# Heads 4 to 7 with the halves of a chunk exchanged over the partitions, in a DeltaNet and SiLU kernel

## The chip, the core and the metric

The kernel runs on one core of a Trainium2 chip. TensorE (PE; its weight loads are listed as PEld), VectorE (DVE), ScalarE (ACT) and GpSimd (POOL) compute, SyncE (SP) issues the DMAs. The metric is the device time of one execution in microseconds. Three runs of the kernel before gave 767.76, 767.8 and 769.63 us, with a median of 767.8 us.

## What is computed

First a recurrent attention block, then a two-layer network on its output. With 4 batches, 8 heads, 768 tokens and head size 48:

```python
k_n = k / (np.linalg.norm(k, axis=-1, keepdims=True) + 1e-06)
for t in range(S):
    y[:, :, t] = q_t @ state                 # state: (B, H, 48, 48)
    v_old = state^T @ k_n_t
    state = state + beta_t * outer(k_n_t, v_t - v_old)
x = y.transpose(0, 2, 1, 3).reshape(3072, 384)
h = x @ w_in                                 # 384 -> 2048
return (h * sigmoid(h)) @ w_out              # 2048 -> 384
```

Everything is in 4-byte floating point.

## The kernel before, in words

**Chunks.** The 768 tokens are cut into 6 chunks (`c`) of 128 tokens. A chunk of one batch (`x`, 0 to 3) is a unit, with all its 8 heads (`h`). Token t of the chunk lies on partition t: the first half of a chunk on partitions 0 to 63 (`lo`), the second on 64 to 127 (`hi`). Within a chunk the recurrence becomes a triangular system over 128 tokens for each head. Its inverse is built from the inverses of the 32x32 blocks on the diagonal (`invert`, L441, a chain of 60 VectorE operations over all heads of a chunk at once, and DMAs before and after it), which `merge` (L526) joins to inverses of 64x64 blocks (`xis`), one for each half. What lies between the halves is applied as a 64x64 product.

**Loads.** `load_k` (L122), `load_q` (L126) and `load_v` (L130) bring one unit with one DMA each, 192 KB, of rows of 192 bytes. All DMAs are issued by SP, in an order fixed in the program (`in_line`). In the built program a DMA also waits until the one eight places before it has landed.

**Scores.** `prepare` (L889) transposes keys and queries (L364), makes the products of all keys with all keys and queries (`score`, L376), scales and masks them into `ap` (ScalarE L397, VectorE L403, with the mask `above`), sends the 32x32 blocks on the diagonal out by four DMAs per unit (`block_out`, L415) and back in by one (`block_in`, L435), scales the keys into `bkb` on GpSimd, loads the keys of the unit that takes this place next, and scales the values on GpSimd.

**Solve.** `solve(c, us)` (L508) is where the change lies. It is a generator. After each of its steps the main loop (from L1047) puts a piece or two of the network of the chunk before it in TensorE's order, so that the one waits while the other computes. `pin` fixes the order of each engine's instructions to that of the program. The steps are:

- `keys(x)` (L551) for the four units, in one step: the product of the old state with the keys. The two heads of a pair lie on the rows 0 to 63 and 64 to 127 of `kq` and of the state, which is block-diagonal, so that one 128x128 product with 96 columns serves both. Four of them fill one PSUM bank `ph` from the pool `psC` (three banks), and VectorE adds it to the values `vs` (L563). In the first chunk there is no old state and no such step.
- `merge`, first and second, a step each.
- Seven rounds, k = 0 to 6. Round k takes `inner(k, lo)` (8 products of 64x64 with 48 columns, rows lo to rows lo), `across(k-1)` (8, rows lo to rows hi) and `inner(k-2, hi)` (8, rows hi to rows hi), as far as these units exist, one product of each in turn (`together`). So rounds 0 to 5 have 8, 16, 24, 24, 16 and 8 products. Each product appears in the profile as two instructions, two passes. After the products: `add(k-1)` on VectorE (64x384), `keep(k)` and `keep(k-2)` on ScalarE (64x384 each, from PSUM into `z`). From round 3 on the round also takes the unit k-3 through `old`, `update` (the new state, L615 and L622) and `new` (the output, L632, L668, L681).

In the main loop `squares` (L284) and `norms` (L301) of the chunk after stand between rounds: after step n = 5 and n = 6, that is after rounds 2 and 3. `norms` is a chain of 15 small VectorE operations (L308 to L326). It gives `n` (what the values are multiplied by) and `g` (what the keys are). The main loop takes two pieces after the two merge steps and one after every other.

**Network.** `hidden` (L724) and, from the second chunk on, `combine` (L810), which makes two 128-token products of the second layer from seven half-size ones; `sum_g` (L798) makes its sums on VectorE, three operations at a time (S3, S4) when `combine` has come to that place. In the first chunk `project` (L748) takes the place of `combine`.

Of the kernel before, what the change touches and what calls it, by code (L numbers as in the profile page):

```python
# [21 lines left out]
def kernel(  # L22
# [91 lines left out]

    def packed(t):
        return t[:].rearrange("p a e w -> p (a e) w")[:, :, 0:D]
# [4 lines left out]

    def load_k(i):  # L122
        if i < N:
            in_line(nc.sync.dma_start(out=packed(kbufs[i % NK]), in_=chunk_of(k, i)))
# [5 lines left out]
    def load_v(i):  # L130
        if i < N and i not in vfs:
            vfs[i] = load.tile([P, H, D], FP32, name="vf", bufs=4)
            in_line(nc.sync.dma_start(out=vfs[i][:], in_=chunk_of(v, i)))
# [118 lines left out]
    )  # L252
    for t in states[: B - 1]:
        nc.gpsimd.memset(t[:], 0.0)
# [21 lines left out]
    def beta_of(c):  # L276
        pb = bank(psA, "a", "pb")
        pin(nc.tensor.transpose(pb[:, 0:BH], beta_fm[:, c * C : (c + 1) * C], ident[0:BH, 0:BH]))
        pin(nc.scalar.activation(out=beta_tok[:, c, :], in_=pb[:, 0:BH], func=ACTF.Copy))
# [21 lines left out]
    def norms(c):  # L301
# [5 lines left out]
        n, g = (small.tile([P, BH], FP32, name=name) for name in ("n", "g"))  # L307
        pin(nc.vector.tensor_scalar(  # L308
# [14 lines left out]
        pin(nc.vector.tensor_scalar(out=n[:], in0=t, scalar1=1e-6, scalar2=None, op0=ALU.add))  # L323
        pin(nc.vector.reciprocal(out=r, in_=n[:]))
# [3 lines left out]
        ))  # L328
        sizes[c], steps[c] = n, g
# [46 lines left out]
    def score(i, u, rooms):  # L376
# [5 lines left out]
        for g, room in enumerate(rooms):  # L382
# [10 lines left out]
            for e in range(2):  # L393
# [7 lines left out]
                for n, (h, at) in enumerate(heads):  # L401
                    j = 1 if n < by_act else 0
                    masked = pin(nc.vector.scalar_tensor_tensor(  # L403
                        out=ap[:, h, j:2, :],
                        in0=pa[e][:, at + j * C : at + 2 * C].rearrange(
                            "p (j t) -> p j t", j=2 - j
                        ),
                        scalar=bt[:, h : h + 1],
                        in1=above[:].unsqueeze(1).to_broadcast([P, 2 - j, C]),
                        op0=ALU.mult, op1=ALU.mult,  # L410
                    ))
# [96 lines left out]
    def solve(c, us):  # L508
# [42 lines left out]
        def keys(x):  # L551

            ph = bank(*CC, "ph")
            for p in range(NP):
                st = states[x][:, p, :].rearrange("p (e w) -> p e w", e=2)[:, :, 0:D]
                pin(nc.tensor.matmul(  # L556
                    ph[:, 2 * D * p : 2 * D * (p + 1)], lhsT=us[x]["kq"][:, p, 0, :], rhs=st,
                    start=(p == 0), stop=True, skip_group_check=True,
                ))
            add(x, slice(0, P), ph[:, 0:DM].rearrange("p (h d) -> p h d", h=H))  # L560

        def add(x, rows, what):
            pin(nc.vector.tensor_tensor(  # L563
                out=vs[x][rows], in0=vs[x][rows], in1=what[rows], op=ALU.add
            ))

        def inner(x, rows):

            if rows == lo:
                pzs[x] = bank(*CC, "pz")[:, 0:DM].rearrange("p (h d) -> p h d", h=H)  # L570
            for h in range(H):
                yield pin(nc.tensor.matmul(  # L572
                    pzs[x][rows, h, :], lhsT=xis[x // HB][rows, x % HB * H + h, :],
                    rhs=vs[x][rows, h, :], start=True, stop=True,
                ))

        def across(x):

            for h in range(H):
                yield pin(nc.tensor.matmul(  # L580
                    pzs[x][hi, h, :], lhsT=us[x]["ap"][lo, h, 0, W:C],
                    rhs=z_of(x)[lo, h // 2, h % 2, 0:D], start=True, stop=True,
                ))
# [5 lines left out]
        def keep(x, rows):  # L589
            pin(nc.scalar.copy(  # L590
                z_of(x)[rows, :, :, 0:D], pzs[x][rows].rearrange("p (a e) d -> p a e d", e=2)
            ))
            if c == 0:
                to = slab[x][rows, D:].rearrange("p (g w) -> p g w", g=2)[:, :, 0 : 2 * (D + GAP)]
                pin(nc.scalar.copy(
                    to.rearrange("p g (h w) -> p g h w", h=2)[:, :, :, 0:D],
                    pzs[x][rows].rearrange("p (g h) d -> p g h d", g=2)[:, :, 1:3, :],
                ))

# [88 lines left out]
        if c > 0:  # L688
            yield
# [7 lines left out]
        for k in range(B + 3):  # L697
# [3 lines left out]
            if k >= 3:  # L701
# [4 lines left out]
                    k < B and inner(k, lo), 0 <= k - 1 < B and across(k - 1),  # L706
                    0 <= k - 2 < B and inner(k - 2, hi),
                ) if part
            ))
            if 0 <= k - 1 < B:  # L710
                add(k - 1, hi, pzs[k - 1])
            if k < B:
                keep(k, lo)
            if 0 <= k - 2 < B:
                keep(k - 2, hi)
# [320 lines left out]
    for n, _ in enumerate(solve(1, us)):  # L1036
        go(pieces, 2 if n in (1, 2) else 1)
        if n == 5:
            squares(2)
        if n == 6:  # L1040
# [6 lines left out]
    for c in range(1, NCH):  # L1047
        if c + 1 < NCH:
# [13 lines left out]
            for n, _ in enumerate(solve(c + 1, us)):  # L1062
                go(pieces, 2 if n in (1, 2) else 1)
                if n == 5 and c + 2 < NCH:
                    squares(c + 2)
                if n == 6 and c + 2 < NCH:
# [36 lines left out]
```

## Time and profile before

| | |
|---|---|
| median of the runs | 767.8 us (767.76 to 769.63) |
| span of the profiled execution, first to last instruction | 766.0 us |
| outside of the span, against the median | 1.8 us |
| TensorE busy | 730.7 us, 95% of the span |
| VectorE busy | 420.2 us, 55% |
| ScalarE busy | 247.2 us, 32% |
| GpSimd busy | 84.4 us, 11% |
| mean granted TensorE clock | 0.981 of full speed |

The profile gives the profiled execution no time of its own but its span; the time around it is taken from the runs. "Busy" counts overlapping instructions once. The mean duration of an instruction is longer than the distance between two starts, since matmuls overlap: a chain of waits, which gives each instruction the time until the next begins, shows the distance. In it "issue" is time in which the engine waited for nothing that the profile shows. A clock of 1.00 is full speed.

### The profile page before, as it was taken

How to read it: one execution, taken by the hardware profiler on the slowest of the kernel's cores; microseconds unless marked ns; L12 is line 12 of the kernel's file. 1: busy time of each engine (PE TensorE's matmuls, PEld its weight loads, DVE VectorE, ACT ScalarE, POOL GpSimd, SP SyncE). 2: the span in 40 equal slices, each digit the busy share in tenths (PEclk: the TensorE clock that was granted, in tenths of full speed). 3: DMA queues.
4: the chain of work that ended last, by engine and by line, in shares of the span. 5: the costliest groups of instructions: out<-in, count | busy, mean ns of one | idle time of the engine just before them, and what ended most of it. 6: DMA issues, size and time to landing. Idle time of an engine off the chain costs nothing.

```text
span 766.0 us, 16569 instructions
## 1 busy us (share of the span) xinstructions
PE 730.7 (95%) x6806; PEld 631.0 (82%) x6806; DVE 420.2 (55%) x1090; ACT 247.2 (32%) x552; POOL 84.4 (11%) x95
## 2 busy tenths in 40 slices
PE   7489899899999999999999999999999999999998
PEld 5256687477778999898999988999987999999987
DVE  6889687872445853555763455673455672321212
ACT  5434466121444122434112434212425212322020
POOL 4005337100021000030000021000012000000000
PEclk9779799999999999999999999999999999999999
DMA  9797445131154022144012044122043013010000
GB/s 176 147 202 218 140 148 109 35 89 20 28 102 79 16 85 34 22 106 80 18 76 43 20 104 78 23 77 43 8 95 67 15 49 70 8 37 1 21 1 21
DMA packets 156283, 51.91 MB, mean 68 GB/s; under 512 B 141840, under 2 KB 148752, under 8 KB 156208
## 3 DMA queue, kind: packets, MB, share of 16 engines
q1 hardware_dynamic: 156208, 50.85, 29.0%
q8 instruction: 54, 0.88, 0.5%
q14 instruction: 21, 0.17, 0.1%
HBM read 34.70 MB, written 14.16 MB: 64 GB/s over the span
## 4 chain that ended last, share of the span: by engine, by line
PE 81%; DVE 10%; DMA 3%; ACT 2%; issue 2%; SPq 1%; POOL 1%; ACTq 0%; DVEq 0%
PE phid L730 31%; PE px L824 13%; PE py L824 11%; PE pa L387 5%; PE pz L572 4%; PE po L753 3%; DVE x L469 3%; DVE rank L465 3%; PE ph L556 2%; PE pt L364 2%; PE pyc L632 2%; PE py L540 2%; PE px L540 2%; PE pyc L604 1%; PE pu L615 1%
## 5 line engine op out<-in xcount | busy, mean ns | idle before, releaser
L730 PE MATMUL phid<-xT,w_in 128*128 128x256 f32 x1152 | 260.7, 382 | 2.2 <-ACT gT L740 1.6
L730 PEld LDWEIGHTS phid<-xT,w_in 128*128 128x128 f32 x1152 | 215.0, 190 | 37.0 <-issue 6.3
L740 ACT ACTIVATE gT<-phid 128x512 f32<-128x512 f32 x96 | 57.2, 597 | 188.7 <-PE phid L730 148.3
L403 DVE SCALAR_TENSOR_TENSOR ap<-pa,g,above 128x128 f32<-128x128 f32 x192 | 58.1, 376 | 41.6 <-ACT ap L397 41.6
L469 DVE TENSOR_TENSOR x<-x,rank 128x30 f32<-128x30 f32 (+9 forms) x180 | 59.7, 332 | 7.4 <-ACT x L458 1.1
L465 DVE TENSOR_TENSOR rank<-g,x 128x30 f32<-128x30 f32 (+9 forms) x180 | 59.4, 330 | 5.0
L806 DVE TENSOR_TENSOR sums_of_g<-gT 128x384 f32<-128x384 f32 (+1 forms) x60 | 29.3, 510 | 58.3 <-ACT gT L740 47.5
L824 PE MATMUL py<-w_out,sums_of_g 128*128 128x192 f32 x320 | 56.8, 329 | 0.0
L824 PE MATMUL px<-sums_of_w,sums_of_g 128*128 128x192 f32 x320 | 56.8, 329 | 0.0
L824 PEld LDWEIGHTS px<-sums_of_w,sums_of_g 128*128 128x128 f32 x320 | 52.2, 190 | 1.4 <-issue 1.4
L824 PEld LDWEIGHTS py<-w_out,sums_of_g 128*128 128x128 f32 x320 | 52.2, 190 | 0.4
L397 ACT ACTIVATE ap<-pa,g 128x128 f32<-128x128 f32 x144 | 41.5, 368 | 30.7 <-PE pa L387 29.7
L426 POOL MEMSET x<- 128x1024 f32 x6 | 5.7, 952 | 405.0 <-DMA xT<-part 403.5
L387 PE MATMUL pa<-kq 48*128 48x256 f32 x384 | 49.7, 390 | 0.2 <-DVE ap L403 0.2
L572 PEld LDWEIGHTS pz<-vf,xi 64*64 64x64 f32 x768 | 38.1, 142 | 13.3 <-issue 7.3
L753 PE MATMUL po<-w_out,gT 128*128 128x384 f32 x128 | 44.7, 495 | 2.9 <-POOL w_out L174 2.9
L572 PE MATMUL pz<-vf,xi 64*64 64x48 f32 x768 | 42.7, 227 | 4.9 <-DVE vf L563 4.4
L387 PEld LDWEIGHTS pa<-kq 48*128 48x128 f32 x384 | 36.2, 186 | 11.5 <-issue 7.8
L563 DVE TENSOR_TENSOR vf<-vf,ph 128x384 f32<-128x384 f32 x20 | 11.1, 554 | 53.1 <-PE ph L556 53.1
L753 PEld LDWEIGHTS po<-w_out,gT 128*128 128x128 f32 x128 | 23.4, 190 | 18.4 <-POOL w_out L174 4.1
L590 ACT COPY z<-pz 64x384 f32<-64x384 f32 x48 | 22.6, 472 | 46.2 <-PE pz L572 40.1
L563 DVE TENSOR_TENSOR vf<-vf,pz 64x384 f32<-64x384 f32 x24 | 13.4, 557 | 42.1 <-PE pz L580 26.1
(134 smaller groups left out, 955.4 us busy)
## 6 DMA issues: line engine op xcount, KB each, us to landing
kb<-in_k_dram SPq DMA_DIRECT2D x24, 192.0 KB, 3.1
z<-in_q_dram SPq DMA_DIRECT2D x24, 192.0 KB, 3.7
vf<-in_v_dram SPq DMA_DIRECT2D x24, 192.0 KB, 3.9
out_dram<-o SPq DMA_DIRECT2D x24, 192.0 KB, 2.0
w_out<-in_moe_w_in_dram SPq DMA_DIRECT2D x4, 768.0 KB, 6.3
blocks<-ap SPq DMA_DIRECT2D x96, 32.0 KB, 1.7
g<-blocks SPq DMA_DIRECT2D x24, 128.0 KB, 2.5
up<-x SPq DMA_DIRECT2D x6, 512.0 KB, 2.6
```

Of the source, the lines that this page charges most:

```text
L387: u["last"] = pin(nc.tensor.matmul(pa[e][:, pp * 2 * C : (pp + 1) * 2 * C], lhsT=kq[rows, 2 * g + pp, 0, :], rhs=kq[rows, 2 * g + pp, :, : ...
L397: copied = pin(nc.scalar.activation(out=ap[:, h, 0, :], in_=pa[e][:, at : at + C], func=ACTF.Copy, scale=bt[:, h : h + 1],))
L403: masked = pin(nc.vector.scalar_tensor_tensor(out=ap[:, h, j:2, :], in0=pa[e][:, at + j * C : at + 2 * C].rearrange("p (j t) -> p j t", j= ...
L465: pin(nc.vector.tensor_tensor(out=tv, in0=g[:, 0:m, m : m + 1].to_broadcast([P, m, n]), in1=x[:, m : m + 1, m + 1 : T].to_broadcast([P, m, ...
L469: yield pin(nc.vector.tensor_tensor(out=x[:, 0:m, m + 1 : T], in0=x[:, 0:m, m + 1 : T], in1=tv, op=ALU.add))
L540: pin(nc.tensor.matmul(pm[to, at : at + T], lhsT=left, rhs=right, start=True, stop=True))
L572: yield pin(nc.tensor.matmul(pzs[x][rows, h, :], lhsT=xis[x // HB][rows, x % HB * H + h, :], rhs=vs[x][rows, h, :], start=True, stop=True,))
L730: pin(nc.tensor.matmul(ph[:, j * GT : (j + 1) * GT], lhsT=w_in[:, a, (2 * f + j) * P : (2 * f + j + 1) * P], rhs=xTs[c, hf][:, a, :], star ...
L740: pin(nc.scalar.activation(out=gTs[f // FG][:, f % FG, :], in_=ph[:], func=ACTF.Silu, scale=0.5))
L753: pin(nc.tensor.matmul(po[:, 0:DM], lhsT=gTs[f // 2 // FG][:, f // 2 % FG, at : at + C], rhs=w_outs[f // HFF][:, f % HFF, :], start=(f == ...
L806: pin(nc.vector.tensor_tensor(out=sums_of_g[:, k, fs], in0=of[0], in1=of[1], op=op))
L824: pin(nc.tensor.matmul(to, lhsT=at, rhs=quarter(f, *b) if isinstance(b, tuple) else sums_of_w[b][:, f], start=start and f == 0, stop=f == ...
```

## The change

Heads 4 to 7 keep keys and values with the two halves of the chunk exchanged over the partitions: their first half is on hi, their second on lo. So "first half" (slot 0) is on lo for heads 0 to 3 and on hi for heads 4 to 7, and slot 1 the other way. `load_k` takes three DMAs per unit and `load_v` four in place of one each. Queries stay as they were. `beta_of` makes four small products in place of one transpose, `norms` three more copies (since `n` is needed in the order of the values, by slots, and `g` in that of the keys), and GpSimd makes a turned mask once. `keys` becomes 16 products of 64x64 with 48 columns per unit, over the four quarters of the array (48 rows lo or hi, columns lo or hi), into two banks, and two VectorE additions of 128x192; its four units are spread over two steps. In a round `inner(k, 0)` and `inner(k-2, 1)` take four heads lo to lo and four hi to hi, `across` four lo to hi and four hi to lo. `add` is one operation of 128x192, and `keep` two copies of 64x192 on ScalarE. `squares` and `norms` move by one step, with the two merges and what is taken after them, so they stay after rounds 2 and 3.

```diff
     def load_k(i):
         if i < N:
-            in_line(nc.sync.dma_start(out=packed(kbufs[i % NK]), in_=chunk_of(k, i)))
+            to = packed(kbufs[i % NK])
+            for s, rows, tokens in ((0, slice(0, P), slice(0, P)), (1, lo, hi), (1, hi, lo)):
+                in_line(nc.sync.dma_start(
+                    out=to[rows, HS * s : HS * (s + 1)], in_=part_of(k, i, s, tokens)
+                ))
...
     def load_v(i):
         if i < N and i not in vfs:
             vfs[i] = load.tile([P, H, D], FP32, name="vf", bufs=4)
-            in_line(nc.sync.dma_start(out=vfs[i][:], in_=chunk_of(v, i)))
+            for slot, rows in ((0, lo), (0, hi), (1, lo), (1, hi)):
+                tokens = hi if slot else lo
+                in_line(nc.sync.dma_start(
+                    out=slots(vfs[i])[rows, slot],
+                    in_=part_of(v, i, int((rows == lo) == (slot == 1)), tokens),
+                ))
...
+        pin(nc.vector.tensor_copy(out=n[0:W], in_=root_of[0:W]))
+        to, of = (x.rearrange("p (b s h) -> p b s h", s=2, h=HS) for x in (n[W:P], root_of[W:P]))
+        for s in range(2):
+            pin(nc.vector.tensor_copy(out=to[:, :, s], in_=of[:, :, 1 - s]))
         sizes[c], steps[c] = n, g
...
-                        in1=above[:].unsqueeze(1).to_broadcast([P, 2 - j, C]),
+                        in1=above_turned[:, j:2, :] if g == 1 else
+                        above[:].unsqueeze(1).to_broadcast([P, 2 - j, C]),
...
         def keys(x):
 
-            ph = bank(*CC, "ph")
+            phs = [bank(*CC, f"ph{e}")[:, 0 : HM].rearrange("p (n d) -> p n d", n=NP) for e in range(2)]
             for p in range(NP):
-                st = states[x][:, p, :].rearrange("p (e w) -> p e w", e=2)[:, :, 0:D]
-                pin(nc.tensor.matmul(
-                    ph[:, 2 * D * p : 2 * D * (p + 1)], lhsT=us[x]["kq"][:, p, 0, :], rhs=st,
-                    start=(p == 0), stop=True, skip_group_check=True,
+                for e, half in ((0, 0), (1, 1), (0, 1), (1, 0)):
+                    rows, cols = slice(W * e, W * e + D), slice(W * half, W * (half + 1))
+                    pin(nc.tensor.matmul(
+                        phs[e][cols, 2 * (p // 2 ^ half) + p % 2, :], lhsT=us[x]["kq"][rows, p, 0, cols],
+                        rhs=states[x][rows, p, W * e : W * e + D],
+                        start=True, stop=True, skip_group_check=True,
+                    ))
+            for e in range(2):
+                to = vs[x][:].rearrange("p (n e) d -> p n e d", e=2)[:, :, e]
+                pin(nc.vector.tensor_tensor(out=to, in0=to, in1=phs[e], op=ALU.add))
...
+        BY_TILE = (0, 4, 1, 5, 2, 6, 3, 7), (4, 0, 5, 1, 6, 2, 7, 3)
...
+        def inner(x, slot):
+
+            if slot == 0:
+                pzs[x] = bank(*CC, "pz")[:, 0:DM].rearrange("p (s h d) -> p s h d", s=2, h=HS)
+            for h in BY_TILE[slot]:
+                rows = half_of(h, slot)
+                yield pin(nc.tensor.matmul(
+                    place(pzs[x][rows], h, slot), lhsT=xis[x // HB][rows, x % HB * H + h, :],
+                    rhs=place(slots(vs[x])[rows], h, slot), start=True, stop=True,
+                    skip_group_check=True,
+                ))
+        def across(x):
+
+            for h in BY_TILE[0]:
+                rows, cols = half_of(h, 0), half_of(h, 1)
                 yield pin(nc.tensor.matmul(
-                    pzs[x][hi, h, :], lhsT=us[x]["ap"][lo, h, 0, W:C],
-                    rhs=z_of(x)[lo, h // 2, h % 2, 0:D], start=True, stop=True,
+                    place(pzs[x][cols], h, 1), lhsT=us[x]["ap"][rows, h, 0, cols],
+                    rhs=z_of(x)[rows, h // 2, h % 2, 0:D], start=True, stop=True,
+                    skip_group_check=True,
                 ))
...
+        def keep(x, slot):
+            for s in range(2):
+                rows = half_of(HS * s, slot)
                 pin(nc.scalar.copy(
+                    packed(z_of(x))[rows, HS * s : HS * (s + 1)], pzs[x][rows, slot]
                 ))
...
         for x in range(B if c > 0 else 0):
             keys(x)
-        if c > 0:
-            yield
+            if x % 2 == 1:
+                yield
...
-                go(pieces, 2 if n in (1, 2) else 1)
-                if n == 5 and c + 2 < NCH:
+                go(pieces, 2 if n in (2, 3) else 1)
+                if n == 6 and c + 2 < NCH:
                     squares(c + 2)
-                if n == 6 and c + 2 < NCH:
+                if n == 7 and c + 2 < NCH:
                     norms(c + 2)
```

## The prediction

> **What bounds the kernel now.** First the page: the span, the slices of TensorE and of its clock.
>
> ```profile
> span 766.0 us, 16569 instructions
> ...
> PE   7489899899999999999999999999999999999998
> ...
> PEclk9779799999999999999999999999999999999999
> ```
>
> From about 165 us on TensorE is full at full clock. Only before that do other things decide. The table by stretches tells it for the solve of chunks 1 and 2:
>
> ```profile
> 178.00:218.00 40.00, 40.00 (x687) 31.07 (x686) 17.64 (x48) 12.82 (x30) 0.00 (x0) 1.00 0.10 24
> ...
> 290.00:333.00 43.00, 42.05 (x738) 38.85 (x737) 22.48 (x60) 15.08 (x36) 0.00 (x0) 1.00 0.14 28
> ```
>
> TensorE is busy for 40.00 of 40.00 and 42.05 of 43.00 us, so what is taken off TensorE here comes off the end, except where it then waits. The chain of waits through the solve of chunk 2 gives the prices (start, time until the next link):
>
> ```profile
> 290.70 3.54 PE ph L556 x32
> ...
> 305.44 1.06 PE pz L572 x16
> 306.50 1.50 PE px L824 x8
> ...
> 309.06 1.50 PE py L824 x8
> ...
> 311.63 1.51 PE py L824 x8
> ...
> 324.25 0.57 DVE vf L563
> 324.82 0.04 issue
> 324.87 1.13 PE pz L572 x16
> ```
>
> The keys of four units take 3.54 us, 111 ns for each of 32 passes. Round 0 (16 passes in one quarter of the array) takes 1.06; round 1 (32 passes in two quarters) runs from 308.00 to 309.06, also 1.06; round 2 (48 passes, three quarters) from 310.56 to 311.63, 1.07. So quarters run beside each other, and a round lasts as long as its fullest quarter: 16 passes, whose starts in the timeline lie 58 ns apart (0.93), and 0.13 of tail. The piece before costs 1.50 where 8 such passes cost 1.30 elsewhere in the chain: 0.20 for going into small products. At round 5 the chain leaves TensorE: VectorE's addition for unit 3 ends late, and by the timeline TensorE waits 1.14 us for it.
>
> **The change part by part.**
>
> *Rounds.* Rounds 0 and 5 spread 16 passes over two quarters, rounds 1 and 4 spread 32 over four: 8 in the fullest. 8 x 58 ns + 0.13 = 0.60 in place of 1.06, 0.46 less. Rounds 2 and 3 keep 16 in lo-lo and in hi-hi, and gain nothing. Four rounds are 1.84 per chunk, 9.2 in chunks 1 to 5. That four quarters keep the 58 ns of three is not in the trace: below, 58 ns is the least that any row shows for such a pass, and above it is 116, if only two run at once. I take 58, as two and three did not differ.
>
> Against this the Trainium skill ("TensorE: Matmul & The Clock Gate", Part 3: Packing small matmuls) states that weight loads overlap running products only where the row groups differ. Here L572 and L580 of round 1 share the rows lo and still had 32 passes in the time of 16, so the row decides; by the rule rounds 1 and 4 would gain nothing, the keys' passes would take twice as long, and the time would be 774.4. The skill ("TensorEngine Tiling (Array Packing)", Gotcha 1) also says that different row tiles can't use one PSUM bank at once, as rounds 0 and 5 now do; the merge L540 does that in its bank, with 128 passes in 2.14 us, and by the rule the time would be 764.6.
>
> *Keys.* 32 passes per unit in four quarters are 8 x 58 = 0.46. But each unit now takes two of the pool's three banks: by the waits of the built program the second product of unit 1 waits for VectorE's first addition of unit 0, and unit 3 for unit 2. In the rows of before an addition starts as the last product ends. From the last weight load of a unit: 0.09 to its product, 0.22 of product (219 ns), 0.35 of addition (352 ns, the 64x192 form L622; before 553), 0.06 to the next load (324.81 to 324.87): 0.72, of which 0.7 is idle. A visit is then 0.20 + 0.46 + 0.7 + 0.46 + 0.13 = 1.95, two are 3.9, against 3.54: 0.3 more per chunk (rounded down, as a few products of unit 1 start before the wait), **+1.5** in five. Without the stall two visits are 2.5, a gain of 1.0 per chunk; with VectorE late by another 0.3 it is a loss of 0.9.
>
> *VectorE between rounds 2 and 5.* Chunk 2 before:
>
> ```profile
> 313.94 1.01 DVE L297 TENSOR_REDUCE ss<-sq 128x8 f32<-128x384 f32 x2 [1.61 <-ACT sq L294]
> ...
> 316.59 0.56 DVE L563 TENSOR_TENSOR vf<-vf,pz 64x384 f32<-64x384 f32 x1
> ...
> 319.45 1.36 DVE L806 TENSOR_TENSOR sums_of_g<-gT 128x384 f32<-128x384 f32 x3
> 320.73 0.17 DVE L308 TENSOR_SCALAR seed<-ss 128x32 uint32<-128x32 uint32 x1
> ```
>
> The extra step moves the pieces one round earlier. In the built order S3 (1.36) then stands ahead of the squares, in the 1.61 us that VectorE idles. That takes 1.36 off the chain before round 5. Against it: three copies in `norms` (0.19 to 0.23 each by its neighbours), 0.6; the addition itself 0.2 less; ScalarE's four copies of 0.31 (the 64x192 copy L595, 0.312) where two took 0.97, 0.27 later, but the squares no longer wait for the `o` copy, so they start 0.4 earlier. Followed from the end of round 2 (311.63), unit 3's addition ends at +12.0 instead of +13.18, TensorE arrives at +11.64 instead of +12.1: a wait of 0.4 in place of 1.14, 0.7 less in chunks 2, 3 and 4, **-2.1**. In chunk 1 no S3 exists; the addition ended 0.6 before TensorE came (210.41 against 211.0). The chain gets 0.95 longer (0.27 twice, 0.6, less 0.2), TensorE 0.46 earlier: a new wait of 0.8, **+0.8**. In chunk 5 `norms` is absent. Queued behind that addition on VectorE are only the state and `xT` copies.
>
> *Start.* SP's first issues and the queue of chunk 1's values:
>
> ```profile
> 1.25 2.79 SPq L124 DMA_DIRECT2D kb<-in_k_dram  x4
> ...
> 108.43 7.33 SPq L133 DMA_DIRECT2D vf<-in_v_dram  x4
> 115.87 2.44 SPq L431 DMA_DIRECT2D blocks<-ap  x4
> ...
> 134.58 1.78 SPq L431 DMA_DIRECT2D blocks<-ap  x4
> ```
>
> An issue that is not held up takes 0.45 (L431, four in 1.78). Twelve key loads are 5.4 in place of 2.79, ahead of the queries. But keys landed 1.18 apart by bytes, which don't change, against 1.35 for three issues: the last keys, the queries and all behind them come about **+0.7** later (0.3 to 1.2). Both the norms and the queries' transposes hang on it.
>
> *Values of chunk 1.* 16 loads follow three big ones. Numbers 9 to 16 wait for the landing of 1 to 8, about 116, so SP is free near 119.6 instead of 115.87. Unit 3's blocks waited until 134.58 for VectorE; three units of 4 issues, a landing, one issue and three key loads (about 5.1 each) put them near 135.5: **+0.9** (0 to 3) on the inverse of chunk 1, which ends the chain there. Later SP needs about 5 of the 5.6 us between units (blocks at 344.48 and 350.06), and the inverse has some 3.6 us of slack, since its last `xe` load lands near 408.4 and the merge starts at 411.99: 0, and up to 1 per chunk if that cover is gone.
>
> *Chunk 0.* Rounds 0 to 3 hide behind VectorE's weight work; rounds 4 and 5 gain 0.46 each, partly taken back by the same work. I take **-0.4** (0 to -1.1).
>
> *The rest at nothing:* beta's products run where TensorE idles 6.80 us behind L279; the masks keep size and count (L403, 376 ns); the four GpSimd copies end, at 0.3 each (the 128x128 select, 0.29), near 6.7, before the mask is needed at 13.73. `keep`'s extra 0.15 lies behind a piece of 1.3.
>
> **Sum:** -9.2 + 1.5 - 2.1 + 0.8 + 0.7 + 0.9 - 0.4 = -7.8. From the span of 766.0 that is 758.2; the median of the runs is 1.8 above the span, so **760.0**.
>
> **Rivals.**
>
> 1. *The keys don't stall*, if VectorE frees the bank before it is needed. For it: VectorE sits idle ahead of each key addition (0.34 us by the timeline). Against: the wait is in the program. Gain 1.0 in place of loss 0.3, five times: 753.5.
> 2. *SP sets the pace.* 48 more key and 72 more value issues, at 0.45 each 54 us on a queue that carries the inverse's transfers. For: SP is ordered, and each unit's blocks stand behind key loads. Against: the slack above. With 1 us per chunk and 3 at chunk 1: about 766.
> 3. *Four quarters run two at a time* (the other side). For: no row shows four. Against: two and three cost the same. Rounds 1 and 4 then stay at 1.06 (+4.6), and a unit's keys take 16 x 58 = 0.93, two visits 5.8 (+9.8 against the forecast): 774.4. It decides from 90 ns per pass on: 240 passes of the fullest quarter (five chunks of 32 + 16) times 32 ns eat the 7.8.
> 4. *The change does not do what it says*, its gains going into waits of the same solve (VectorE at round 5 in all chunks): 767.8.
>
> **How the numbers follow.** Forecast 0.66 (756 to 765), rival 1 0.13, rival 2 0.08, rival 3 0.08, rival 4 0.05. 0.3% (2.3 us) is what a measurement can tell from no change. Faster, below 765.5: forecast, rival 1 and half of rival 2, 0.83; within: the other half and rival 4, 0.09; slower: rival 3, 0.08. The range goes down to rival 1 with a little more from chunk 0, 752.5, and up to rival 2, 766.
>
> **What would show it.** Rounds 0, 1, 4 and 5 of chunks 1 to 5 at 0.60; rounds 2 and 3 at 1.06; two key visits near 1.75 to 1.95, each with one idle stretch of 0.7 released by VectorE; the wait at round 5 near 0.4 in chunks 2 to 4, and a new one in chunk 1; the first scores 0.7 later; the restart after the inverse of chunk 1 later than 164.8. It is wrong if passes in a quarter lie more than 58 ns apart with four running, or if merges wait for `xe` or `xi`.

## The result, and the profile after

The kernel after takes 800.0 us (median of four runs, 796.9 to 801.0), the kernel before 767.8 us on the same chip: a ratio of 1.041, 95% interval 1.039 to 1.044. The change makes it 4.1% slower, where 760.0 (752.5 to 766) was forecast. The profiled execution took 796.9 us, 1.7 of them outside its span. Its page, with the rows that were read first for the kernel before:

```profile
span 795.2 us, 17917 instructions
...
PE   6747899888999699999799999899999999999998
...
PEclk7868899999999899999989999999999999999999
```

TensorE is no longer full: beside a worse start it has holes in slices 14, 20 and 26, one per chunk, and the clock dips in slices 14 and 21. To see where the 29 us went, each span is cut at TensorE's first score product (the start of `prepare`) and at its first keys product (the start of `solve`) of each chunk, read off the timelines. "One load" is the experiment e1 and "e12" the last one, both below:

| stretch, us | before | after | one load | e12 |
|---|---|---|---|---|
| to the first scores | 11.3 | 14.9 | 11.2 | 12.5 |
| chunk 0, to the scores of chunk 1 | 95.4 | 104.3 | 92.5 | 96.2 |
| chunk 1, scores to keys | 71.2 | 76.8 | 71.6 | 71.8 |
| solve of chunk 1 (keys to next scores) | 45.9 | 44.4 | 44.4 | 44.4 |
| chunk 2, scores to keys | 66.8 | 74.7 | 66.9 | 67.6 |
| solve of chunk 2 | 49.6 | 47.2 | 47.3 | 47.6 |
| chunk 3, scores to keys | 66.8 | 74.5 | 66.9 | 66.9 |
| solve of chunk 3 | 49.6 | 47.3 | 47.3 | 47.4 |
| chunk 4, scores to keys | 66.8 | 72.0 | 66.9 | 66.9 |
| solve of chunk 4 | 49.6 | 47.3 | 47.3 | 47.2 |
| chunk 5, scores to keys | 66.8 | 66.9 | 66.9 | 66.9 |
| keys of chunk 5 to the end | 126.2 | 124.8 | 124.8 | 124.8 |
| the span (the rows are rounded) | 766.0 | 795.2 | 753.9 | 760.2 |

So the part that the change is about does what was forecast: the five solves (the last of them in the last row) are 10.0 us shorter. The loss, 39 us, lies where no product was changed, between the start and the solve of chunk 1 (18) and between scores and keys of chunks 2 to 4 (21). The table by stretches shows the same for chunk 2, first of the kernel after (columns: stretch, its length, then busy time and instructions of PE, PEld, DVE, ACT and POOL, then clock, DMA share and GB/s), then of the kernel before:

```profile
240.50:315.20 74.70, 68.54 (x376) 60.57 (x375) 40.87 (x118) 19.69 (x47) 8.55 (x10) 0.95 0.32 68
315.20:362.40 47.20, 46.36 (x875) 42.21 (x874) 24.29 (x72) 17.16 (x46) 1.64 (x3) 1.00 0.17 34
```

```profile
223.70:290.50 66.80, 66.80 (x375) 59.47 (x375) 41.35 (x118) 19.92 (x47) 8.14 (x10) 1.00 0.33 75
```

Nearly the same instructions, but TensorE idles for 6.2 of the 74.7 us, and the clock falls to 0.95 with it, which goes with the rest of the 7.9. TensorE's and ScalarE's timelines of the kernel after give the wait (start, duration, what, and in brackets the idle time ahead of it):

```profile
261.63 9.44 PE L792 MATMUL phid<-xT,w_in 128*128 128x256 f32 x43
277.23 4.30 PE L886 MATMUL px<-w_out,gT 128*128 128x192 f32 x16 [6.16 <-ACT gT L802]
```

```profile
265.93 0.60 ACT L802 ACTIVATE gT<-phid 128x512 f32<-128x512 f32 x1 [1.99 <-PE phid L792]
276.08 0.60 ACT L505 COPY x<-g 128x128 f32<-128x128 f32 x2 [9.55 <-DMA kb<-in_k_dram]
276.59 1.08 ACT L802 ACTIVATE gT<-phid 128x512 f32<-128x512 f32 x2
```

TensorE waits for `gT`, which ScalarE makes from TensorE's own products. ScalarE could make it at once, but works in order, and ahead of it stands a copy that begins the inverse (L505), which waits 9.55 us for the blocks `g`. (The row names a key load; the load of `g` for the last unit was issued at 273.36, just ahead of those keys, and is what the copy reads; in e4, below, the same wait of that copy, 6.65 us, is put down to `g` itself.) In the kernel before the copy and the product came without such a wait:

```profile
250.27 0.64 ACT L458 COPY x<-g 128x128 f32<-128x128 f32 x2 [0.45 <-DMA g<-blocks]
254.21 2.76 PE L824 MATMUL px<-w_out,gT 128*128 128x192 f32 x16
```

The blocks are late because of SP. Its timeline in chunk 2, after and then before:

```profile
240.93 10.70 SPq L152 DMA_DIRECT2D vf<-in_v_dram  x16
...
252.39 3.21 SPq L478 DMA_DIRECT2D blocks<-ap  x4
256.81 0.32 SPq L486 DMA_DIRECT2D g<-blocks  x1
257.24 1.78 SPq L139 DMA_DIRECT2D kb<-in_k_dram  x3
259.11 2.03 SPq L478 DMA_DIRECT2D blocks<-ap  x4
```

```profile
222.88 3.41 SPq L133 DMA_DIRECT2D vf<-in_v_dram  x4
...
228.07 1.99 SPq L431 DMA_DIRECT2D blocks<-ap  x4
231.65 0.32 SPq L439 DMA_DIRECT2D g<-blocks  x1
232.08 0.39 SPq L124 DMA_DIRECT2D kb<-in_k_dram  x1
```

16 value loads hold SP for 10.70 us, 0.67 each, where 4 took 3.41. TensorE's first score came 16.7 us later than before (240.5 against 223.75), the first blocks 24.3 (252.39 against 228.07). And behind each unit's blocks three key loads take 1.78 in place of 0.39. Then the blocks of a unit follow each other by 5.5 to 6.7 us, as far apart as the scores themselves (5.6 before), so SP never makes up for the late start.

### The profile page after: what moved, and what is told of

Same layout as the page of the kernel before. It is cut to its first block, busy times and chain, and to the rows that moved or that the text cites. A ratio compares the mean times of both kernels' runs of the same rounds, so it can differ in the third digit from the quotient of the medians.

```text
span 795.2 us, 17917 instructions
## 1 busy us (share of the span) xinstructions
PE 733.1 (92%) x7328; PEld 624.4 (79%) x7328; DVE 413.6 (52%) x1128; ACT 253.1 (32%) x596; POOL 85.3 (11%) x99
## 4 chain that ended last, share of the span: by engine, by line
PE 58%; DMA 2%; SPq 2%; issue 1%; ACT 0%; DVE 0%; DVEq 0%
PE phid L792 20%; PE px L886 14%; PE py L886 10%; PE pa L433 3%; PE pyc L694 2%; PE pyc L666 2%; PE pz L631 2%; PE pt L410 1%; PE py L587 1%; PE px L587 1%; DMA blocks<-ap 1%; PE ph L604 1%; PE pu L677 1%; SPq L478 1%; SPq L139 1%
## 5 line engine op out<-in xcount | busy, mean ns | idle before, releaser
L868 DVE TENSOR_TENSOR sums_of_g<-gT 128x384 f32<-128x384 f32 (+1 forms) x60 | 29.2, 509 | 56.4 <-ACT gT L802 46.0
L449 DVE SCALAR_TENSOR_TENSOR ap<-pa,g,above 128x128 f32<-128x128 f32 x96 | 30.2, 377 | 43.4 <-ACT ap L443 43.4
L433 PE MATMUL pa<-kq 48*128 48x256 f32 x384 | 51.4, 402 | 0.3 <-DVE ap L449 0.2
L886 PE MATMUL px<-w_out,gT 128*128 128x192 f32 x160 | 33.9, 374 | 14.2 <-ACT gT L802 14.2
L611 DVE TENSOR_TENSOR vf<-vf,ph 128x192 f32<-128x192 f32 x40 | 12.4, 351 | 61.4 <-PE ph L604 41.7
L886 PEld LDWEIGHTS px<-w_out,gT 128*128 128x128 f32 x160 | 31.2, 221 | 15.7 <-ACT gT L802 15.4
L296 PE MATMUL pw<-state,ident 128*128 128x384 f32 x80 | 32.9, 559 | 4.0 <-DVE state L162 2.8
L654 ACT COPY z<-pz 64x192 f32<-64x192 f32 x96 | 28.9, 313 | 23.7 <-PE pz L631 14.8
```

The costliest lines, as they stand in the source:

```text
L296: done = pin(nc.tensor.matmul(pw[:, 0:DM], lhsT=ident[:], rhs=states[B - 1][:].rearrange("p a w -> p (a w)")[:, 0:DM], start=True, stop=Tr ...
L433: u["last"] = pin(nc.tensor.matmul(pa[e][:, pp * 2 * C : (pp + 1) * 2 * C], lhsT=kq[rows, 2 * g + pp, 0, :], rhs=kq[rows, 2 * g + pp, :, : ...
L449: masked = pin(nc.vector.scalar_tensor_tensor(out=ap[:, h, j:2, :], in0=pa[e][:, at + j * C : at + 2 * C].rearrange("p (j t) -> p j t", j= ...
L654: pin(nc.scalar.copy(packed(z_of(x))[rows, HS * s : HS * (s + 1)], pzs[x][rows, slot]))
L868: pin(nc.vector.tensor_tensor(out=sums_of_g[:, k, fs], in0=of[0], in1=of[1], op=op))
L886: pin(nc.tensor.matmul(to, lhsT=at, rhs=quarter(f, *b) if isinstance(b, tuple) else sums_of_w[b][:, f], start=start and f == 0, stop=f == ...
```

## The experiments

Two theories were tested. **A:** the added DMA issues on SP are the whole loss, because of what is queued behind them. **B:** something else in the change delays the inverse (three more small copies, turned masks, longer key additions, ScalarE's copies). Later ones concern what in the issues costs: their place, their number or their form.

**One load, and the kernel before with many.** e1 takes the change and gives it the loads of the kernel before; e2 takes the kernel before and cuts its loads:

```diff
 e1, in the kernel after
-            for s, rows, tokens in ((0, slice(0, P), slice(0, P)), (1, lo, hi), (1, hi, lo)):
-                in_line(nc.sync.dma_start(out=to[rows, HS * s : HS * (s + 1)], ...
+            in_line(nc.sync.dma_start(out=packed(kbufs[i % NK]), in_=chunk_of(k, i)))
...
-            for slot, rows in ((0, lo), (0, hi), (1, lo), (1, hi)):
...
+            in_line(nc.sync.dma_start(out=vfs[i][:], in_=chunk_of(v, i)))
 e2, in the kernel before
+            for s, rows, tokens in ((0, slice(0, P), slice(0, P)), (1, lo, lo), (1, hi, hi)):
...
+            for s in range(2):
+                for rows in (lo, hi):
...
```

> The kernel after, with one DMA per unit for keys and for values as in the kernel before. It leaves out the exchange of the halves in the data of heads 4 to 7; every compute instruction stays. Theory A (the added DMA issues on SP are the whole loss: a load of half the heads holds SP for 0.61 us and the gap to the next is 0.045, where the forecast took 0.45; the inverses come late, ScalarE's gT copies behind them, and TensorE waits): the 39.2 us that the kernel after lost outside its solves of chunks 1 to 5 (18.2 ahead of the keys of chunk 1 and 21.0 between later scores and keys) go, the 10.0 that those solves gained stay, so 756 to 758 us. Theory B (something else in the change delays the inverses: the three more copies of the norms, the turned masks, the longer keys on VectorE or the two copies of ScalarE): most of the loss stays, 785 to 800. Between these the time says what share the DMAs have.

> The kernel before, with its key loads cut into three DMAs per unit and its value loads into four, of the same sizes as in the kernel after but each to the rows where the tokens were before; nothing else changes. Theory A: the same 39 us are lost, less what hides because the solves are longer here: 800 to 812 us. Theory B: the DMAs alone cost at most a few us, 768 to 773.

e1: 760.3 us (755.6 to 764.3, four runs), ratio to before 0.990 (0.985 to 0.995); the profiled run is the fastest of the four. e2: 797.1 us, ratio 1.038 (1.036 to 1.040). Theory B falls: with every compute instruction of the change and the old loads, the stretches between scores and keys are back at 66.9 us (see the table); with the old computing and the new loads the kernel before is slowed by 29 us. The row of e1 that answers to the one above:

```profile
219.70:286.60 66.90, 66.90 (x375) 59.34 (x375) 41.13 (x118) 19.93 (x47) 8.14 (x10) 1.00 0.34 75
```

e2 lost less than the 32 us or more expected of it. Its stretches from scores to keys in chunks 3 and 4 are 70.2 and 69.7, where the kernel after has 74.5 and 72.0, and its solves are 2.4 longer. In the solve SP is busy too, with `xT` and the queries, and a longer solve leaves it less far behind at the next scores. The rows agree for chunks 2 and 3: SP issues the last `g` load 31.7 and 29.2 us after the first score product in e2, 32.9 and 31.4 in the kernel after, and TensorE's wait for `gT` is 4.96 and 2.47 in place of 6.16 and 4.81. Some 3 us of what e2 lost less lie in chunk 0 (5.9 over the kernel before, against 8.9), which this does not explain.

**Keys or values.** e3 keeps the three key loads and takes one for the values, e4 the other way.

> The kernel after with its three key loads per unit but one value load per unit (heads 4 to 7 then multiply values of the wrong halves). Theory A in parts: the keys cost 4.9 us at the start (the first key loads end 4.95 later in the profile) and up to 4 more ahead of the inverse of chunk 1, and 0 to 1 in each later chunk, where three key loads stand ahead of a unit's blocks: 762 to 772 us. Theory B: 785 to 800.

> The kernel after with its four value loads per unit but one key load per unit (heads 4 to 7 then use keys of the wrong halves). Theory A in parts: the values of chunk 0 stand ahead of the store of the inverse (8.5 us), those of chunk 1 ahead of its blocks (5), those of chunks 2 to 4 ahead of theirs (5 to 8 each, three times): 780 to 793 us. With e3 the two losses add to about 39 over e1, or to less where both hide in the same slack. Theory B: 785 to 800, and then e3 as much.

e3: 765.7 us, ratio 0.996 (0.994 to 0.998), as expected. e4: 771.3, ratio 1.004 (1.003 to 1.006), 9 us below the range expected. Over e1, whose median is known to some 4 us by its interval, that is 5 and 11 us, 16 together, but both in one kernel cost 40. The two are not independent, and e7 asks how.

**Keys out of the way.** e7 issues the key loads of a chunk behind its last unit's blocks, where SP then waits for the inverse; the values stay:

```diff
             scale(i)
-            load_k(i + B)
             size(i)
+            if b == B - 1:
+                for n in range(B):
+                    load_k((c + 1) * B + n)
             yield
```

> The kernel after with only the key loads of a chunk's scores moved behind its last unit's blocks; the values stay where they were, ahead of the first unit's. It asks why e3 (keys split) costs about 6 and e4 (values split) about 12 over e1, but both together about 40. Theory A: ahead of the first blocks SP is 8.5 us late by the values; with three key loads between the units it needs 5.6 us for a unit, as much as TensorE does for its scores, and stays late; without them it needs about 4.1 and catches up some 1.5 us per unit, so the later chunks lose 0 to 3 us each in place of 5 to 8, as in e4, and the start costs 4.9 more than there: 770 to 780 us. Rival A3 (the sum is larger because the DMA engines or the landings are fuller with both): about 790 or more.

771.3 us (766.4 to 773.7), ratio 1.004 (1.002 to 1.006), in theory A's range, near its lower end. SP in chunk 2:

```profile
230.08 10.70 SPq L152 DMA_DIRECT2D vf<-in_v_dram  x16
...
241.54 2.74 SPq L478 DMA_DIRECT2D blocks<-ap  x4
245.48 0.32 SPq L486 DMA_DIRECT2D g<-blocks  x1
245.92 1.83 SPq L478 DMA_DIRECT2D blocks<-ap  x4
249.03 0.31 SPq L486 DMA_DIRECT2D g<-blocks  x1
249.44 1.85 SPq L478 DMA_DIRECT2D blocks<-ap  x4
```

The values take their 10.70 us as before, and the first blocks are as late. But units now follow each other by 3.5 to 4.4 us on SP, and the lateness of the blocks behind their scores, 7.3 us over the kernel before at the first unit, is down to 2.0 at the fourth (253.05): scores to keys takes 66.9 to 67.1 us in chunks 2 to 5. This is why keys and values together cost more than their sum: the values make SP late, the keys take away the time in which it caught up.

**Everything out of the way.** e5 moves the keys like e7 and the values behind them, e6 also gives eight of the first twelve key loads to ScalarE's queue:

```diff
             if b == B - 1:
                 for n in range(B):
                     load_k((c + 1) * B + n)
+                for n in range(B):
+                    load_v(c * B + n)
+                for n in range(B):
+                    size(c * B + n)
```

> The kernel after with all its 7 part loads per unit, only issued at other places: in a chunk's scores the keys of the next chunk and the values of this one stand behind the last unit's blocks, where SP waits some 30 us for the inverse; the values of chunk 0 stand behind the stores of the inverse of chunk 0 (two units) and behind the loads of its blocks (two). The first twelve key loads stay. Theory A (the loss is what these issues hold up on SP, the blocks of each chunk): the losses between scores and keys go (21.0) and most of the 18.2 ahead of chunk 1 but the 4.9 of the start: 760 to 766 us. A rival, A2 (the part loads cost by themselves, in DMA engines or at the readers, wherever they are issued): 780 to 795.

> As e5_loads_moved, and of the first key loads those of heads 4 to 7 are issued by ScalarE, which has nothing to do until keys have landed. Theory A: the first scores come at 11 to 12 us instead of 14.9, and the time is 3 to 5 us below that of e5_loads_moved: 756 to 762 us. A2: no difference from e5_loads_moved.

794.2 us, ratio 1.035 (1.032 to 1.037), and 792.1, ratio 1.032 (1.029 to 1.034): both expectations of A missed by 28 us or more, and A2 named a number like this. TensorE's waits from the scores to the keys of chunk 1 in e5 tell another cause:

```profile
PE po L820 <- POOL w_out L196: 23.1, 1, 23.1
```

GpSimd scales the values as soon as they land, and works in order too. In chunk 1 the narrowing of a weight of the second layer stood behind that scaling, and TensorE behind the weight. In chunks 2 to 5, without narrowing, scores to keys took 67 to 69 us. So the edit had only moved the queue from SP to GpSimd. In e6, ScalarE's eight issues took 6.2 us ahead of its table load, and the first scores came at 12.5 in place of 15.0.

**Mending that.** e9 puts the scaling of chunk 1's values behind the narrowing, and of chunk 0's values loads two units where they were and two behind the inverse's stores. e10 gives ScalarE four of the first key loads, behind its table load.

> e5_loads_moved lost its gain in chunk 1 alone: there GpSimd's scaling of the values waited 19.9 us for the late values, with the narrowing of the second layer's weights queued behind it, and TensorE waited 23.2 us for that weight; its later periods from keys to keys are 115.1 to 115.7 us, where the kernel after has 119 to 122. Here the scaling of chunk 1's values stands behind the narrowing, and of chunk 0's values two units are loaded where they were and two behind the stores of the inverse. All 7 part loads per unit are kept. Theory A (place, not number): the 23.2 us go and some of the start, 762 to 769 us. A2 (part loads cost by themselves): over 780.

> As e9_loads_placed, and of the first twelve key loads ScalarE issues four (the last half of each unit), behind its table load, which in e6 stood 6.2 us behind eight such issues. Theory A: the first keys are complete some 2 us earlier and the inverse of chunk 0 with them; 1 to 4 us below e9_loads_placed: 759 to 766 us. A2: as e9.

e9: 768.9 us, ratio 1.002 (1.000 to 1.003). e10: 766.7, ratio 0.999 (0.998 to 1.001), 0.7 over its range. The 23 us are gone. What is left over e1 lies mostly in chunk 1, where scores to keys take 76.7 us in e10 and 71.6 in e1: TensorE's longest wait for `gT` is 3.94 in place of 1.92, and the clock is 0.96 in place of 1.00. The later chunks lose 0.3 to 1.3 each. One new cost shows in VectorE's inverse, which takes 32.4 us from the issue of the last blocks' load in chunk 2 where e7 takes 29.8. VectorE in e10 while GpSimd scales (one scaling runs from 263.64 for 1.03 us):

```profile
263.59 0.40 DVE L514 TENSOR_TENSOR rank<-g,x 128x228 f32<-128x228 f32 x1
264.02 0.91 DVE L518 TENSOR_TENSOR x<-x,rank 128x228 f32<-128x228 f32 x1
264.96 0.40 DVE L514 TENSOR_TENSOR rank<-g,x 128x234 f32<-128x234 f32 x1
```

An operation of 0.40 takes 0.91 beside the scaling. Three of the chunk's four scalings do this to the inverse, and the fourth to a sum of the network (1.99 in place of 1.36). How much of the lost time this makes was not measured by itself.

**The best of both.** e12 takes the start and chunk 0 of e10 and from chunk 1 on the order of e7.

> e7_keys_moved lost nothing from chunk 1's scores on (its periods from scores to keys are 66.8 to 67.2 us, those of e1_one_load 66.9), and e10_placed_act_start is 8.3 us earlier than it at the first scores of chunk 1, but then loses 5 in chunk 1 and 1 to 2 in each later chunk, where GpSimd scales the late values beside VectorE's inverse (29.5 us from its first copy of the blocks in place of 27.4). This kernel has the start and chunk 0 of e10 and from chunk 1 on the order of e7: keys behind the last unit's blocks, values ahead of the first. All 7 part loads per unit are kept. Theory A (place and catching up decide): 756 to 762 us, 1 to 4 above e1_one_load's fastest run, and faster than the kernel before by 0.7 to 1.4%. A2 (part loads cost by themselves): no better than e10, 765 or more.

760.7 us (758.5 to 762.1), ratio 0.991 (0.988 to 0.994). This version has the change whole, with all seven loads per unit, and is faster than both kernels, than the one before by 0.9%. Its page:

```profile
span 760.2 us, 17911 instructions
...
PE   7639899899999999999999999999999999999998
```

The holes are gone but for the start. Place decides nearly all: the same loads cost 40 us over e1 in the kernel after, and here the medians do not differ (760.7 against 760.3), as far as e1's interval of some 4 us tells. In the profiled runs e12 is 6.4 us longer than e1, 5 of them ahead of the scores of chunk 1.

**Number or form.** In the kernel after, from chunk 1 on, a unit's first key load (128 rows, four heads) holds SP for 0.39 us and the other two (64 rows, four heads each) for 0.61 each. e13 has as many loads at the same places, but all over 128 rows and fewer heads:

```diff
-            for s, rows, tokens in ((0, slice(0, P), slice(0, P)), (1, lo, hi), (1, hi, lo)):
+            for heads in (slice(0, 4), slice(4, 6), slice(6, 8)):
...
-            for slot, rows in ((0, lo), (0, hi), (1, lo), (1, hi)):
+            for h in range(0, H, 2):
```

> The kernel after with as many loads, 3 for the keys and 4 for the values of a unit, at the same places, but each over all 128 rows and fewer heads (4, 2, 2 and 2, 2, 2, 2); it leaves out the exchange of the halves in the data of heads 4 to 7. In the kernel after the key load over 128 rows holds SP for 0.39 us and the two over 64 rows for 0.61 each, all with the same heads. The forecast had 0.45 an issue. Theory C (the number was harmless at the price forecast; the price of loads over 64 rows made the loss): 16 values take 7 us instead of 10.7, a unit's cycle on SP 5.1 instead of 5.6, so it catches up again; the start is held by bytes; 764 to 776 us. Theory D (the number alone is too much at any such price): 785 or more. Rival E (the issue price goes by the number of loads or of bytes and is 0.6 here too): the time of the kernel after, 795 to 800.

771.7 us (766.5 to 776.5), ratio 1.006 (1.003 to 1.009): theory C, within its range. SP in chunk 2:

```profile
233.65 8.21 SPq L150 DMA_DIRECT2D vf<-in_v_dram  x16
241.96 0.41 SPq L819 DMA_DIRECT2D out_dram<-o  x1
242.48 1.89 SPq L475 DMA_DIRECT2D blocks<-ap  x4
245.57 0.32 SPq L483 DMA_DIRECT2D g<-blocks  x1
246.00 1.46 SPq L138 DMA_DIRECT2D kb<-in_k_dram  x3
```

Sixteen loads take 8.21 in place of 10.70, three 1.46 in place of 1.78. With a load at 0.47 instead of 0.61, 28 of the 40 us over e1 go; the 11 that stay, to some 4 us by e1's interval, go with the number. The form of the load is not the whole price, though. At the start of the kernel after, where the twelve key loads follow each other, those over 128 rows take 0.60 to 0.61 too when they stand behind a load of 64 rows (the fourth, at 3.18 us, takes 0.61). The loads of 64 rows took 0.60 or more wherever they stood. e13 has none of them, so it does not tell the two effects apart.

**What the rounds need.** e11 is e10 with the products of one quarter in a row, instead of the two quarters in turn:

```diff
-        BY_TILE = (0, 4, 1, 5, 2, 6, 3, 7), (4, 0, 5, 1, 6, 2, 7, 3)
+        BY_TILE = (0, 1, 2, 3, 4, 5, 6, 7), (4, 5, 6, 7, 0, 1, 2, 3)
```

> As e10_placed_act_start, with the heads of a round in another order: the four products of one quarter one after the other, then the four of the other, instead of in turn. It asks what the 0.60 us of a round need. Theory Q (passes run beside each other only where those next to each other in the order go to different quarters): rounds 0 and 5 go from 0.60 back towards 1.06 us, about 0.9 more per chunk, and 4 to 5 us in the whole. Rival (the quarters are fed independently of the order): 0.60 in each and the same time.

782.5 us (782.1 to 783.7), 15.8 above e10, three times what was expected. The chain of waits of e11 in chunk 2 has round 0 at 0.87:

```profile
317.66 0.87 PE pz L635 x16
318.53 1.50 PE py L890 x8
```

and rounds 1, 2 and 3, by the starts around them, at 0.88, 1.80 and 1.80 (0.61, 1.10 and 1.10 in the kernel after). So it is neighbours in the order that go to different quarters which run beside each other; where they go to the same one, little of the overlap is left (0.87, where 16 passes in one quarter took 1.06). The forecast priced rounds by their fullest quarter alone; that held here because `together` and `BY_TILE` take the quarters in turn.

## Why the prediction was wrong, point by point

- **Rounds, -9.2: right, about -8.5.** The chain of waits of the kernel after in chunk 2:

```profile
315.27 0.68 PE ph L604 x32
315.99 0.37 DVE vf L611
...
316.40 0.68 PE ph L604 x30
...
331.75 0.60 PE pz L631 x16
332.35 1.50 PE py L886 x8
...
348.91 0.60 PE pz L631 x16
```

  Rounds 0 and 5 take 0.60, rounds 1 and 4 take 0.61 (333.85 to 334.46; 344.42 to 345.03), as forecast from 58 ns a pass; rounds 2 and 3 went from 1.07 to 1.10. Between starts round 5 went from 1.06 to 0.67 in e1; the six rounds together are 1.7 us shorter per chunk. Four quarters do run beside each other. The Trainium skill's rule in "TensorE: Matmul & The Clock Gate" (Part 3: Packing small matmuls), that loads overlap products only in other row groups, does not hold here: round 1 has two quarters on each half of the rows, and the measurement decides. The two quarters of rounds 0 and 5 write one PSUM bank from different rows, and at 0.60 they overlap too. So rival 3 falls.
- **Keys, +1.5: right, about +1.9.** The stall is there, so rival 1 falls: from the last weight load of unit 0 to the first of unit 1 it is 0.68 us (315.72 to 316.40), mostly VectorE's addition, where 0.72 was forecast. Two visits are 3.64 (the first of e1 from 286.67 to 288.49, 1.82) against 3.54. From the first keys product to round 0, less 1.30 for every six or eight products of the network between, e1 takes 8.70 and the kernel before 8.33: 0.37 more per chunk, 0.1 in the visits and the rest in pieces that take up to 0.2 longer behind small products.
- **VectorE between rounds 2 and 5, -2.1 and +0.8: right in direction, too cautious.** In e1 the addition of unit 3 ends at 320.16 and round 5 starts at 320.33: the whole wait of 1.14 is gone in chunks 2 to 4, not 0.7 of it. The new wait in chunk 1 did not come; no wait of TensorE for that addition is in the solve of e1's chunk 1. Rounds, keys and VectorE together were forecast at -9.0 in the five solves, and measured at -10.0, in parts about -8.5, +1.9 and -3.1 to -3.4.
- **Start, +0.7: wrong, 3.6.** The twelve first key loads hold SP for 7.74 us, not 5.4, and bytes do not cover it: the DMA engines are busy for 0.48 of the first 10 us, where they were full (1.08) before. The inverse of chunk 0 ends 4.9 later. Behind it the values of chunk 0, 16 loads for 12.61 us, hold up the store of the inverse (issued at 63.83, though VectorE was done at 59.6). That was not counted: the forecast looked for such a queue in chunk 1 alone, and took chunk 0 at -0.4; it lost 8.9.
- **Values of chunk 1, +0.9: wrong, 5.6** from scores to keys.
- **Later, "0, and up to 1 per chunk if that cover is gone": wrong, 7.9, 7.7 and 5.2.** This is the step that failed, with three errors in it. It followed SP's cycle between units alone: the 16 values ahead of a chunk's first blocks, 10.70 us where there were 3.41, are counted for chunk 1 and not after it. Even at the price of e13 they take 8.21, which is 4.8 more than before, and chunk 2 of e13 loses 2.3 from scores to keys. "An issue that is not held up takes 0.45 (L431)" priced the new loads by the block stores, which cover 32 rows and are another form; the rows of before had no load of 64 rows, and its neighbours (L124 at 0.39, L133 at 0.85 each) gave an upper end of 0.85 that the range did not take in. And the "3.6 us of slack" was read at the end of the inverse, where the merge follows, while what is short first is at its beginning. In the kernel before ScalarE's first copy of the inverse ran at 250.27 and the product behind its `gT` at 254.21. After, the copy comes 25.8 later and that product was ready to start at 271.07, 16.9 later: 8.95 late, 6.16 waited, so the cover was 2.8 us.
- **Rival 2 (SP sets the pace) was the true one, at 0.08 and about 766.** It had the queue, but the wrong price, and not its main lever: the cycle per unit on SP, about 5 us in the forecast, came to 5.5 us beside the 5.6 of TensorE's scores, so SP hardly catches up. With the price that the forecast used (e13, 0.47) the time is 771.7: 28 us nearer, and still above the range, so the price was not the only error.
- **Rival 4** (no gain in the solves) falls with the solves.
- **Chance.** That e1's median, 760.3, is near the 760.0 of the forecast does not confirm the sum: e1 has none of the +1.6 that the forecast counted for the loads, its solves gain 1.0 more, chunk 0 gains 3.0 in its profile where 0.4 was forecast, and its runs differ by up to 9 us.

One rule spoke against the loads and was not weighed. The Trainium skill ("DMA: Bandwidth & Descriptors", Rules for kernel authors) advises against two transfers to disjoint halves of the partitions in place of one over all 128. The runs agree with the advice where the loads stand in the way of the blocks (e1 against the kernel after); in e12 they cost little. Its reason, that such transfers serialize on the same engines, is not what binds here: while SP issues the 16 values of chunk 2 the DMA share is 0.49, against 0.93 with 4 loads in the kernel before.

Open: why a load of 64 rows holds SP longer than one of 128, and why one of 128 rows does behind it. Why e2 loses 11 us less than the kernel after loses over e1 is shown in part by SP's rows and TensorE's waits in chunks 2 and 3, was not tried by itself, and is open for chunk 0.

## What to carry to other kernels

When a change cuts one transfer into several, price the issues by a row of the same form, and follow the in-order queue that they go through to whoever stands behind them: here SP's blocks, then ScalarE's first copy of the inverse, then TensorE. Slack is to be read at the first consumer in that order, and a queue that only just keeps pace never makes up for a late start. Where the issues can be put at a time in which the queue is idle, they cost little (e12); but see whose in-order queue is waiting for the data then (e5).

## What the runs showed of the hardware beside that

- A DMA issue on SP did not go by its bytes alone: with rows of 192 bytes, 128 rows of four or eight heads took 0.39 us (keys, behind a load of another kind), 128 rows of two heads 0.47 (values, e13), 64 rows of four heads 0.61 (keys and values), and 128 rows of four heads behind such a load 0.60 to 0.61 as well (the start of the kernel after). On ScalarE's queue eight loads of 64 rows took 6.18 us with the gaps between them, 0.60 to 0.74 each (e6). The Trainium skill ("DMA: Bandwidth & Descriptors", Issuing engines are not separate DMA queues) calls the sequencer's time for an issue usually small beside the transfer; here 16 transfers were bound by it.
- GpSimd's scaling of 128x384 values holds up VectorE's operations on SBUF: 0.91 in place of 0.40 us (e10). The Trainium skill ("SBUF — State Buffer", SBUF: two separate sides) describes such a lock between these two engines; the row agrees with it.
- Runs of one kernel scatter with the granted clock: e1 ran at 755.6 us with a mean granted clock of 0.986 and at 764.3 with 0.970. Between the profiles of different kernels, one each, it differs most in chunk 0 (0.89 in e1, 0.86 before, 0.79 after); what sets it was not tried.
